# An attention and a feed-forward kernel: other loads, other engines and another order for batch 0

## The chip, the cores and the metric

The kernel runs on one core of a Trainium2 chip. The core has TensorE (PE, matmuls; PEld, the loading of their weights), VectorE (DVE), ScalarE (ACT), GpSimd (POOL) and SyncE (SP), and 16 DMA engines that all queues share. The metric is the time of one execution in device microseconds, the median of several runs. A profile comes from one further execution; its span is measured from the first instruction to the last.

## The reference

For each of 8 batches and 8 heads there are 576 tokens of 64 numbers in `q`, `k` and `v`, in fp32. `w_phi` is 64 x 128.

```python
def phi(x):
    proj = np.einsum('bhsd,df->bhsf', x, w_phi)
    proj = proj - np.max(np.abs(proj), axis=-1, keepdims=True)
    return np.concatenate([np.exp(proj), np.exp(-proj)], axis=-1)
q_p, k_p = phi(q), phi(k)
kv = np.einsum('bhsf,bhsd->bhfd', k_p, v)
z = np.sum(k_p, axis=2)
num = np.einsum('bhsf,bhfd->bhsd', q_p, kv)
den = np.einsum('bhsf,bhf->bhs', q_p, z)[..., None] + 1e-06
x = num / den                       # heads side by side: 4608 tokens x 512
out = (np.maximum(x @ w_gate, 0) * (x @ w_val)) @ w_out   # d_ff = 1536
```

## The kernel before

Every step of the work is a small function `do_xx`, and one long string, `ORDER`, lists the calls in the order in which they are issued. A word such as `ke.0.1.3.0:5@kp0` is step `ke` with arguments (batch 0, group of heads 1, chunk 3, sign 0), which works on PSUM bank 5 and takes slot 0 of the ring of buffers `kp`. Each engine takes its own instructions in the order of the words, and semaphores between the engines follow from the data. So the string sets what is queued behind what, on each engine, and on the DMA queues of SP, ACT and POOL.

The 576 tokens of a batch are split: 512 of them in four chunks of 128, and the last 64, which are packed with those of other heads or of another batch. Heads are loaded and worked on in three groups, (0,1), (2,3,4) and (5,6,7). For a group the steps are:

- `lk`, `lq`, `lm`, `ln` load k, q and the remainders on POOL's queue and turn fp32 into bf16 on the way. `lv` loads v; of batch 0 on POOL's queue, of the others on SP's. `lw` loads v's remainders on SP. `wl` and `wo` load thirds of the feed-forward weights on POOL's queue (`wl.0` is w_val, `wl.1` w_gate). `wp` and `wq` load w_phi on SP in two layouts, a 32-row and a 64-row one, and `wc` and `wd` turn them into bf16 on DVE.
- k is turned. In batch 0 TensorE does it (`k0`, transposes against the identity made by `id`, then the copy `k1` on DVE, then the product with w_phi, `k2`); in later batches DVE's 32x32 transposes do it (`kt`, `ku`, then the product `kr`). q is turned by DVE in all batches (`qt`), and its product with w_phi is `qc`, or in batch 0 eight separate `qs`, of 32 rows each.
- ACT takes the exponentials of both signs (`ke` for k, L563; `qe` for q, L709). DVE takes the maxima of the absolute values (`kx`, L571; `qx`, L717). The scale that follows from k's maxima (`kk`, `kp`) goes into v: `vs` on POOL (L618), `vd` and `vp` on DVE, `vr` for v's remainder on POOL (L637, four calls a batch), `vo` for the column of ones.
- `kv` (L658) is the product of k's features with v, and `kc` or `kd` copies it out. `qy`, `qz`, `qu`, `qw` turn q's maxima into scales. `nu` (L757) is the product of q's features with kv; `nt`, `nv`, `nr`, `nx` (L778, L788, L796, L800) add the two signs, divide, and leave 128 tokens of x. `xp` turns x on TensorE and `xa` or `xc` copies it; later `xt` turns it by DMA.
- The feed-forward part: `pv`, `pg` (L945) for quarters of batch 0, `fv`, `fg` (L916) for 512 tokens at once, `va`, `vb`, `pa`, `pc` copy the value on ACT or DVE, `ga`, `pb` (L937, L966) multiply with the gate; `fo`, `fp` (L977, L1006) are the last product, `oc`, `oe` copy it and `od` stores it from SP.

`zz.n` issues n matmuls on a tile of zeros, on whatever bank the word names; nothing reads them. `gt.0` loads a few bytes from k of batch 0 on SP, so that what SP issues later waits for them.

The end of the string starts the last products; ahead of them, for most of the time, the words interleave the feed-forward part of one batch with the attention of the next.

Of the kernel before, what the change touches and what calls it, by code (L numbers as in the profile page):

```python
# [1066 lines left out]
```

## Time and profile before

| | |
|---|---|
| runs | 379.55, 379.31, 379.26 us; median 379.31 |
| profiled execution | 378.79 us, span 376.8 |
| granted TensorE clock, mean | 0.986 |
| TensorE busy | 367.3 us (97%) |
| DVE, ACT, POOL busy | 296.3, 222.6, 161.4 us |
| DMA | 38.04 MB moved |

The profiled execution took 2.0 us more than its span, and 0.5 less than the median of the runs. A matmul's busy time is modelled and overlaps its neighbours, so 97% is not 97% of the peak rate. Idle time of an engine other than the one that sets the end costs nothing by itself.

### The profile page before, as it was taken

The page shows a single profiled execution, that of the slowest core. Times are in us where ns is not written, and L with a number is a line of the kernel's source. Part 1 is how long each engine was busy: PE and PEld are TensorE (multiplying, and loading weights), DVE is VectorE, ACT ScalarE, POOL GpSimd, SP SyncE. Part 2 cuts the span into 40 slices and gives each one's busy share as a digit, 9 for nine tenths or more (in the row PEclk, how much of TensorE's full clock was granted, in tenths as well). Part 3 has the DMA queues.
Part 4 walks back from the last instruction along what each step waited for, and adds up shares of the span by engine and source line. Part 5 has one row for each costly group of instructions (what it writes and reads, how often), then busy time and mean ns, then how long its engine had stood idle before and what let it go on. Part 6 is the DMA issues. An engine that isn't in the chain of part 4 may idle for free.

```text
span 376.8 us, 9181 instructions
## 1 busy us (share of the span) xinstructions
PE 367.3 (97%) x3591; PEld 197.2 (52%) x3591; DVE 296.3 (79%) x680; ACT 222.6 (59%) x539; POOL 161.4 (43%) x180
## 2 busy tenths in 40 slices
PE   8788999999999999999999999999999999999996
...
PEclk9859999999999999999999999999999999999999
DMA  9999999699954664289713944193400021301122
...
DMA packets 90513, 38.04 MB, mean 101 GB/s; under 512 B 64230, under 2 KB 85734, under 8 KB 90470
## 3 DMA queue, kind: packets, MB, share of 16 engines
...
q10 hardware_dynamic: 144, 0.13, 0.1%
q14 instruction: 15, 0.12, 0.1%
...
## 4 chain that ended last, share of the span: by engine, by line
PE 89%; DVE 5%; ACT 4%; DMA 2%; issue 0%; SPq 0%; DVEq 0%; ACTq 0%
PE bank L916 46%; PE bank L977 22%; PE bank L658 6%; PE bank L757 4%; PE bank L945 4%; PE bank L694 3%; ACT kp L563 2%; PE bank L511 2%; DMA w64f<-in_w_phi_dram 2%; DVE mk L571 1%; ACT qp L709 1%; PE bank L1006 1%; PE bank L898 1%; DVE u L788 1%; DVE maxq L717 1%; DVE t L778 1%
## 5 line engine op out<-in xcount | busy, mean ns | idle before, releaser
L563 ACT ACTIVATE kp<-bank 128x384 bf16<-128x384 f32 x192 | 83.2, 513 | 26.2 <-PE bank L511 15.0
L977 PE MATMUL bank<-wo,h 128*128 128x512 bf16 x420 | 98.3, 379 | 0.0
L937 DVE SCALAR_TENSOR_TENSOR h<-bank,val 128x512 bf16<-128x512 f32 x100 | 66.3, 681 | 29.8 <-PE bank L916 25.5
L916 PE MATMUL bank<-xTs,wg 128*128 128x512 bf16 x352 | 86.7, 379 | 0.0
L916 PE MATMUL bank<-xTs,wv 128*128 128x512 bf16 x352 | 86.2, 379 | 0.0
L800 POOL TENSOR_TENSOR xu<-u,r 128x512 bf16<-128x512 f32 x36 | 37.5, 1044 | 97.3 <-DVE r L796 92.4
L931 ACT CAST val<-bank 128x512 bf16<-128x512 f32 x70 | 41.6, 606 | 62.2 <-PE bank L916 50.8
L709 ACT ACTIVATE qp<-bank 128x512 bf16<-128x512 f32 x128 | 70.9, 632 | 10.1 <-DVE maxq L717 5.1
L618 POOL TENSOR_TENSOR vs<-vn,ek 128x780 bf16<-128x780 f32 (+3 forms) x40 | 53.0, 1338 | 37.8 <-ACT ek L580 35.1
L977 PEld LDWEIGHTS <-h 128*128 128x128 bf16 x420 | 39.1, 98 | 44.0 <-issue 0.9
L916 PEld LDWEIGHTS <-wv 128*128 128x128 bf16 x400 | 37.0, 98 | 43.2 <-issue 3.5
L916 PEld LDWEIGHTS <-wg 128*128 128x128 bf16 x400 | 37.4, 98 | 42.0 <-issue 1.8
L571 DVE TENSOR_REDUCE mk<-bank 128x3 f32<-128x384 f32 x96 | 49.0, 539 | 4.3 <-ACT kp L563 2.2
L717 DVE TRANSPOSE_TENSOR_REDUCE maxq<-bank 128x16 f32<-128x512 f32 x64 | 42.3, 692 | 3.5 <-PE bank L694 2.3
L986 ACT COPY ob<-bank 128x512 f32<-128x512 f32 x23 | 13.6, 593 | 37.5 <-PE bank L977 37.2
L788 DVE TENSOR_TENSOR u<-bank,t 128x195 f32<-128x195 f32 (+1 forms) x108 | 33.4, 330 | 1.9
L778 DVE TENSOR_TENSOR t<-bank,cq 128x195 f32<-128x195 f32 (+1 forms) x96 | 29.8, 327 | 5.0 <-PE bank L757 4.1
L757 PEld LDWEIGHTS <-qp 128*128 128x128 bf16 x512 | 24.1, 98 | 13.6 <-issue 2.0
L757 PE MATMUL bank<-kv,qp 128*128 128x65 bf16 x512 | 27.2, 194 | 1.2 <-ACT qp L709 0.8
L934 DVE CAST val<-bank 128x512 bf16<-128x512 f32 x30 | 20.2, 678 | 8.4 <-PE bank L916 8.3
L658 PEld LDWEIGHTS <-kp 128*128 128x128 bf16 x640 | 24.0, 101 | 3.7 <-DVE h L937 0.3
L658 PE MATMUL bank<-vs,kp 128*128 128x65 bf16 x512 | 24.2, 199 | 0.0
...
## 6 DMA issues: line engine op xcount, KB each, us to landing
...
```

The costliest lines, as they stand in the source:

```text
L563: nc.scalar.activation(kp_of(3 * b + j)[:, i, s].rearrange("p n f -> p (n f)"), bank[bk[0]][:, 0 : 3 * F], AF.Exp, scale=(1.0, -1.0)[s],)
L571: nc.vector.tensor_reduce(mk_of(3 * b + j)[:, :, i], bank[bk[0]][:, 0 : 3 * F].rearrange("p (n f) -> p n f", f=F), axis=AX.X, op=ALU.max, ...
L618: nc.gpsimd.tensor_tensor(vs_of(3 * b + j)[:, s, 0:n].rearrange("p n i e -> p (n i) e")[:, :, 0:e], src[:, lo:hi].rearrange("p h i e -> p ...
L658: nc.tensor.matmul(out_ps[:, h - lo, s, :], lhsT=lhsT, rhs=rhs, start=(at == 0), stop=(at == 2 * n * (C + 1) - 1),)
L709: nc.scalar.activation(qp_of(4 * b + i)[:, s, 4 * hq : 4 * hq + 4].rearrange("p h m -> p (h m)"), bank[bk[0]], AF.Exp, scale=(1.0, -1.0)[s],)
L717: nc.vector.tensor_reduce(maxq[:, :, i, 4 * hq : 4 * hq + 4].rearrange("p t h -> p h t"), bank[bk[0]].rearrange("p (h t u) -> p h t u", h= ...
L757: nc.tensor.matmul(bank[bk[0]][:, E * n : E * (n + 1)], lhsT=qp_of(4 * b + i)[:, s, h, :], rhs=kv_of(b)[:, h, s, :],)
L800: eng.tensor_tensor(xu_of(n).rearrange("p (h d) -> p h d", d=D), u_of(n)[:, :, 0:D], r_of(n).to_broadcast([P, H, D]), op=ALU.mult,)
L916: nc.tensor.matmul(bank[bk[0]], lhsT=w[:, dc, P * f : P * f + P], rhs=xT(g)[:, dc, :], start=(dc == 0), stop=(dc == NDC - 1),)
L931: nc.scalar.copy(val_of(NFC * g + f), bank[bk[0]])
L937: nc.vector.scalar_tensor_tensor(h2_of(g, f), bank[bk[0]], 0.0, val_of(NFC * g + f), op0=ALU.max, op1=ALU.mult)
L977: nc.tensor.matmul(bank[bk[0]], lhsT=h2_of(g, f)[:, P * t : P * t + P], rhs=wo_sb[:, f, :], start=(f == 0), stop=(f == NFC - 1),)
```

## The change

Nearly the whole string stands in another order, and some steps are replaced:

- k's group 1 of batch 0 (heads 2 to 4) is loaded by SP as fp32 (`lf`, into the space of `xT_mix`), and turned into bf16 by DVE (`cf.0`, two heads) and ACT (`cg.1`, one head), where `lk.0.1` did both on POOL's queue.
- w_phi is loaded once (`wr`, on ACT's queue, 64-row layout). Its 32-row copy is made by TensorE (`w1`, two matmuls with the selection matrix `sel`, which `sl` makes on DVE from the identity) and copied by ACT (`wa`). `wp`, `wq`, `wc` go.
- q of batch 0 is turned by TensorE (`q0`, 16 transposes in all) and copied by DVE (`q1`), and its product with w_phi is `qb`, eight matmuls of 64 rows and 512 columns, in place of `qt` and `qs` (16 matmuls of 32 rows and 512 columns). Tokens of a tile of batch 0 are then every fourth token, so `od` of batch 0 stores rows with a stride.
- `vr` (four calls a batch) becomes `vq` (two calls a batch of twice the size), in all batches.
- The matmuls on zeros are 71 in 14 places in place of 62 in 5; nearly all write bank 1.
- `id` comes ahead of POOL's first load. `wl.0.1` comes ahead of two of the three loads of v of batch 0; `lk.1.3` and `lq.1.2` ahead of two `vs`; `wl.1.0` behind all `vs` of batch 0. `gt.0` goes; a `gt.1`, which reads the buffer `kT`, stands near the end. A few copies change between ACT and DVE.

The string up to the first `pv`, before and after:

```diff
-ms.0 ms.2 ms.3@vr0 lk.0.1 ms.6 wp wq ms.4@vr1 wd ms.5 lq.0.1 wc id if zz.37:0 k0.1:0 k1.1:0@kT0
-zz.5:1 k2.1:0123 lk.0.2 ke.0.1.1.0:1@kp0 ke.0.1.2.0:2 ke.0.1.3.0:3 ke.0.1.0.0:0 qt.0.1@qT0
-ke.0.1.3.1:3 kx.0.1.1:1@mk0 lk.0.0 kx.0.1.2:2 ke.0.1.2.1:2 ke.0.1.1.1:1 lm.0.1 zz.6:4 k0.2:4
-k1.2:4@kT0 zz.7:5 k2.2:4567 ke.0.2.2.0:6@kp1 kx.0.1.3:3 ke.0.2.3.1:7 lm.0.0 lq.0.0 kx.0.1.0:0
-kx.0.2.0:4@mk1 ke.0.1.0.1:0 lw.0.0 k0.0:2 k1.0:2@kT0 zz.7:1 k2.0:2013 kk.0.1.1@ek0 ke.0.2.1.1:5
-qt.0.0@qT1 kx.0.2.3:7 ke.0.2.2.1:6 kx.0.2.2:6 kx.0.0.0:2@mk2 lv.0.1 ke.0.0.2.1:1@kp2 ke.0.2.1.0:5
-lm.1.0 lv.0.0 ke.0.0.3.1:3 ke.0.0.1.0:0 ke.0.2.0.0:4 lv.0.2 ke.0.0.0.1:2 kk.0.1.0 lm.1.1 wl.1.0
-kx.0.2.1:5 kp.0.2.1:7 ke.0.0.0.0:2 ke.0.2.0.1:4 lw.0.1 qs.0.1.0:6 kx.0.0.1:0 kx.0.0.3:3 qx.0.1.0:6
-vs.0.1.1@vs0 kp.0.2.0:7 qs.0.0.1:5 qe.0.0.1.0:5@qp0 gt.0 lk.1.3 qs.0.0.2:2 lv.1.2 kx.0.0.2:1
-ke.0.2.3.0:7 vp.2:7@vs1 kk.0.0.1@ek1 vs.0.1.0 ke.0.0.2.0:1 qs.0.0.0:4 wl.0.1 kk.0.0.0 ke.0.0.3.0:3
-qx.0.0.0:4 qx.0.0.2:2 vo.0@vs2 vd.0.2.0:7 ke.0.0.1.1:0 qs.0.1.1:1 qe.0.0.1.1:5 qe.0.0.0.1:4@qp1
-qx.0.1.1:1 qs.0.1.2:3 qe.0.1.2.0:3@qp2 qe.0.0.0.0:4 qs.0.0.3:0 qe.0.0.3.0:0@qp3 wl.0.0 qe.0.1.0.0:6
-qs.0.1.3:4 qx.0.0.1:5 qe.0.0.3.1:0 vd.0.2.1:7 qe.0.1.0.1:6 qe.0.1.1.0:1 vr.0.0.0 vr.0.0.1 qy.0.0:5
-qx.0.1.2:3 vr.0.1.0 qx.0.1.3:4 vr.0.1.1 kv.0.2:7 kc.0.2:7@kv0 vo.1 kv.0.1:6 qz.0.0:5@my0 qu.0.0@mz0
-qw.0.0@cq0 qx.0.0.3:0 kt.1.1@kT0 nu.0.0.2:7 nt.0.0.2:7@t0 qe.0.1.3.1:4 qy.0.1:0 qz.0.1:0@my0
-vs.0.0.1 kc.0.1:6 ku.1@kT1 vs.0.0.0 kv.0.0:5 qe.0.1.3.0:4 nu.0.0.1:6 nt.0.0.1:6@t1 kc.0.0:5
-qe.0.0.2.0:2 qu.0.1@mz0 qw.0.1 qy.0.2:0 qe.0.1.1.1:1 nv.0.0.1:6@u0 qe.0.1.2.1:3 qy.0.3:4 nu.0.0.0:5
-nt.0.0.0:5@t2 qe.0.0.2.1:2 nv.0.0.2:7 nv.0.0.0:5 nr.0.0@r0 nu.0.1.1:1 qz.0.2:0@my0 qu.0.2@mz0 lv.1.0
-nt.0.1.1:1@t2 qz.0.3:4@my0 nu.0.1.2:5 qw.0.2 nv.0.1.1:1@u1 lq.1.2 nt.0.1.2:5@t0 kr.1.1:7630
-nx.0.0@xu0 ke.1.1.3.1:0@kp2 wl.1.1 ke.1.1.0.0:7 nu.0.1.0:2 nt.0.1.0:2@t2 nu.0.2.0:4 xp.0.0:1
-xa.0.0:1 nv.0.1.2:5 nv.0.1.0:2 wo.0 nu.0.2.1:5 nr.0.1@r0 nx.0.1@xu0 kx.1.1.3:0@mk2 wl.0.2 nu.0.2.2:2
-lm.2.0 nt.0.2.1:5@t2 ke.1.1.3.0:0 nt.0.2.2:2@t0 nt.0.2.0:4@t1 ke.1.1.1.1:6 lm.2.1 qu.0.3@mz0
-kx.1.1.2:3 pv.1.0:1 pa.1.0:1@val0 ke.1.1.1.0:6 nv.0.2.0:4@u1 nv.0.2.1:5 nv.0.2.2:2 nr.0.2@r0
 ...
+ms.0 ms.3@vr0 wr ms.5 ms.4@vr1 id sl lf cf.0 if wd lk.0.2 cg.1 zz.17:0 k0.1:0 k1.1:0@kT0 lq.0.0
+lm.0.0 lk.0.0 lm.0.1 zz.2:1 w1:2 lq.0.1 lm.1.1 wa:2 zz.2:1 k2.1:0345 ke.0.1.3.0:5@kp0 kx.0.1.1:3@mk0
+ke.0.1.2.1:4 lv.0.1 k0.2:2 kx.0.1.3:5 ke.0.1.0.1:0 kx.0.1.2:4 k1.2:2@kT1 ke.0.1.3.1:5 wl.0.1
+ke.0.1.2.0:4 zz.3:1 q0.0:6 lv.0.0 ms.2 q1.0:6@qT0 zz.4:1 k2.2:4257 ke.0.1.1.1:3 zz.2:1 k0.0:6
+ke.0.1.0.0:0 kx.0.2.1:2@mk1 lv.0.2 ke.0.1.1.0:3 ke.0.2.0.1:4@kp1 ke.0.2.1.1:2 kx.0.1.0:0 k1.0:6@kT1
+kk.0.1.1@ek0 kx.0.2.3:7 kx.0.2.0:4 lw.0.0 kk.0.1.0 ke.0.2.1.0:2 ke.0.2.2.1:5 ke.0.2.3.1:7 zz.8:1
+k2.0:6032 ke.0.0.3.1:2@kp2 kx.0.2.2:5 ke.0.2.0.0:4 zz.7:1 q0.1:4 kx.0.0.2:3@mk0 kx.0.0.3:2
+ke.0.2.2.0:5 qb.0.2:5 lm.1.0 kx.0.0.1:0 ke.0.0.2.0:3 q1.1:4@qT1 ke.0.0.3.0:2 vs.0.1.0@vs0 lw.0.1
+ke.0.0.2.1:3 ke.0.0.1.0:0 vo.1 kp.0.2.1:7 lk.1.3 kp.0.2.0:7 ke.0.0.1.1:0 zz.2:1 qb.0.0:2 kx.0.0.0:6
+qb.1.0:4 qe.0.1.0.1:4@qp0 lq.1.2 vs.0.1.1 qx.0.0.2:5 ke.0.2.3.0:7 ke.0.0.0.1:6 kk.0.0.1@ek1
+vs.0.0.1@vs1 kk.0.0.0 vo.0 vq.0.1 qe.0.1.0.0:4 qe.0.0.2.1:5@qp1 qb.1.1:3 qx.0.0.0:2 qx.0.1.1:3
+vp.2:7@vs2 qe.0.1.1.0:3@qp2 zz.2:1 qb.0.1:0 qx.0.0.1:0 qx.0.1.0:4 ke.0.0.0.0:6 qe.0.0.2.0:5
+qe.0.0.1.0:0 vd.0.2.0:7 vq.0.0 lw.1.0 zz.15:1 qy.0.0:4 qz.0.0:4@my0 zz.2:1 qb.0.3:6 qe.0.1.1.1:3
+vd.0.2.1:7 qb.1.3:5 qe.0.0.0.1:2 qu.0.0@mz0 lw.1.1 qb.1.2:4 qx.0.1.3:5 qe.0.0.1.1:0 qe.0.0.0.0:2
+zz.3:1 kv.0.1:3 qx.0.0.3:6 qx.0.1.2:4 kc.0.1:3@kv0 qe.0.0.3.1:6@qp3 kv.0.2:0 qy.0.3:3 nu.0.0.1:2
+qw.0.0@cq0 kc.0.2:0 wl.0.0 vs.0.0.0 kv.0.0:7 wl.1.0 qe.0.1.2.0:4 kc.0.0:7 lv.1.2 lv.1.3 kt.1.1@kT1
+qy.0.2:0 nt.0.0.1:2@t0 qz.0.3:3@my0 qe.0.0.3.0:6 nv.0.0.1:2@u0 qz.0.2:0@my1 qy.0.1:3 qz.0.1:3@my2
+nu.0.0.2:1 nt.0.0.2:1@t0 nu.0.0.0:0 qu.0.1@mz0 nt.0.0.0:0@t1 nv.0.0.2:1 nv.0.0.0:0 nr.0.0@r0
+nx.0.0@xu0 qe.0.1.3.1:5 zz.2:2 kr.1.1:7236 qe.0.1.2.1:4 qu.0.2@mz1 nu.0.1.2:1 qw.0.1 qe.0.1.3.0:5
+nu.0.1.1:0 kx.1.1.2:3@mk0 lv.1.0 nt.0.1.2:1@t1 nu.0.1.0:4 nt.0.1.0:4@t0 xp.0.0:5 nt.0.1.1:0@t2
+ke.1.1.1.1:2@kp2 ke.1.1.2.1:3 nv.0.1.0:4@u0 lv.1.1 qu.0.3@mz0 wl.1.1 nv.0.1.1:0 nu.0.2.1:4
+nu.0.2.2:0 qw.0.2 nv.0.1.2:1 nr.0.1@r0 nt.0.2.1:4@t1 nt.0.2.2:0@t2 nv.0.2.1:4@u1 nu.0.2.0:1
+nt.0.2.0:1@t0 nx.0.1@xu0 nv.0.2.2:0 nv.0.2.0:1 wl.0.2 ke.1.1.1.0:2 xa.0.0:5 pv.1.0:5 ke.1.1.2.0:3
 ...
```

The functions:

```diff
@@ -343,11 +342,11 @@
     xT_all = sb.tile([P, 4, NDC, SF], BF16, name="xTs", tag="xTs")
     xT_mix = sb.tile([P, NDC, SF], BF16, name="xTm", tag="xTm")
     h2 = sb.tile([P, NH2, SF], BF16, name="h2", tag="h2")
-    w32f = sb.tile([P, 2, F], FP32, name="w32f", tag="w32f")
     w64f = sb.tile([P, F], FP32, name="w64f", tag="w64f")
     w32 = sb.tile([P, 2, F], BF16, name="w32", tag="w32")
     w64 = sb.tile([P, F], BF16, name="w64", tag="w64")
     ident = sb.tile([P, P], BF16, name="ident", tag="ident")
+    sel = sb.tile([D, 2, P], BF16, name="sel", tag="sel")
     identf = sb.tile([P, P], FP32, name="identf", tag="identf")
     zero = sb.tile([P, 256], BF16, name="zero", tag="zero")
     mark = sb.tile([P, D], BF16, name="mark", tag="mark")
@@ -369,17 +368,33 @@
 
 
 
-    def do_wp(bk):
-        nc.sync.dma_start(
-            out=w32f.rearrange("p a f -> p (a f)"),
-            in_=w_phi.rearrange("(r a) f -> r (a f)", a=2)[None].to_broadcast([4, R, 2 * F]),
-        )
+    def do_sl(bk):
+        nc.vector.tensor_copy(
+            sel.rearrange("d a (i r) -> d a i r", r=R),
+            ident[0:D, 0:D].rearrange("d (r a) -> d a r", a=2)[:, :, None, :].to_broadcast([D, 2, 4, R]),
+        )
+
+    def do_w1(bk):
+        for a in range(2):
+            nc.tensor.matmul(
+                bank[bk[0]][:, F * a : F * (a + 1)],
+                lhsT=sel[:, a, :],
+                rhs=w64[0:D, :],
+                start=(a == 0),
+                stop=(a == 1),
+            )
 
     def do_wq(bk):
         nc.sync.dma_start(out=w64f, in_=w_phi[None].to_broadcast([2, D, F]))
 
+    def do_wr(bk):
+        nc.scalar.dma_start(out=w64f, in_=w_phi[None].to_broadcast([2, D, F]))
+
     def do_wc(bk):
-        nc.vector.tensor_copy(w32.rearrange("p a f -> p (a f)"), w32f.rearrange("p a f -> p (a f)"))
+        nc.vector.tensor_copy(w32.rearrange("p a f -> p (a f)"), bank[bk[0]][:, 0 : 2 * F])
+
+    def do_wa(bk):
+        nc.scalar.copy(w32.rearrange("p a f -> p (a f)"), bank[bk[0]][:, 0 : 2 * F])
 
     def do_wd(bk):
         nc.vector.tensor_copy(w64, w64f)
@@ -419,6 +434,31 @@
             in_=k[b, lo:hi, 0:SF, :].rearrange("h (p c) d -> p h c d", c=C),
         )
 
+    def k_first():
+        flat = xT_mix.rearrange("p a b -> p (a b)").bitcast(FP32)[:, 0 : 3 * C * D]
+        return flat.rearrange("p (h x) -> p h x", h=3)
+
+    def do_lf(bk):
+        lo, hi = HEADS[1]
+        nc.sync.dma_start(
+            out=k_first().rearrange("p h (c d) -> p h c d", d=D),
+            in_=k[0, lo:hi, 0:SF, :].rearrange("h (p c) d -> p h c d", c=C),
+        )
+
+    def cast_first(copy, half):
+        lo, hi = ((0, 2), (2, 3))[half]
+        at = HEADS[1][0]
+        copy(
+            kn_of(0)[:, at + lo : at + hi].rearrange("p h c d -> p h (c d)"),
+            k_first()[:, lo:hi],
+        )
+
+    def do_cf(bk, half):
+        cast_first(nc.vector.tensor_copy, half)
+
+    def do_cg(bk, half):
+        cast_first(nc.scalar.copy, half)
+
     def do_lq(bk, b, hq):
         lo, hi = (4 * hq, 4 * hq + 4) if hq < 2 else (0, H)
         nc.gpsimd.dma_start(
@@ -461,9 +501,18 @@
                 in_=v[b, :, P * i : P * i + P, :].rearrange("h p d -> p h d"),
             )
 
+    def do_lu(bk, i):
+        lo, hi = HEADS[i]
+        nc.sync.dma_start(
+            out=v_flat()[:, lo:hi],
+            in_=v[0, lo:hi, 0:SF, :].rearrange("h (p c) d -> p h c d", c=C),
+        )
+
     def do_gt(bk, j):
 
-        nc.sync.dma_start(out=mark[0:1], in_=kn_of(0)[0:1, HEADS[j][0], 0, :])
+        nc.sync.dma_start(
+            out=mark[0:1], in_=kT_of(j).rearrange("p n m a -> p (n m a)")[0:1, 0:D]
+        )
 
     def do_lw(bk, b, hh):
         nc.sync.dma_start(
@@ -638,6 +687,15 @@
             vr_of(b)[r, s, :, hh, :],
             vm_of(b)[r],
             ek_of(3 * b)[r, s, 0, :][:, :, None].to_broadcast([SM, 4, E]),
+            op=ALU.mult,
+        )
+
+    def do_vq(bk, b, hh):
+        r = slice(SM * hh, SM * (hh + 1))
+        nc.gpsimd.tensor_tensor(
+            vr_of(b)[r, :, :, hh, :],
+            vm_of(b)[r][:, None, :, :].to_broadcast([SM, 2, 4, E]),
+            ek_of(3 * b)[r, :, 0, :][:, :, :, None].to_broadcast([SM, 2, 4, E]),
             op=ALU.mult,
         )
 
@@ -679,6 +737,30 @@
 
 
 
+    def do_q0(bk, hq):
+        pt = bank[bk[0]].bitcast(BF16)
+        for n in range(8):
+            h, cp = 4 * hq + n // 2, n % 2
+            nc.tensor.matmul(
+                pt[:, P * n : P * n + P],
+                lhsT=qn_of(0)[:, h, 2 * cp : 2 * cp + 2, :].rearrange("p c d -> p (c d)"),
+                rhs=ident,
+                is_transpose=True,
+            )
+
+    def do_q1(bk, hq):
+        nc.vector.tensor_copy(
+            qT_of(hq).rearrange("p h m a -> p (h m a)"), bank[bk[0]].bitcast(BF16)
+        )
+
+    def do_qv(bk, hq):
+        nc.scalar.copy(qT_of(hq).rearrange("p h m a -> p (h m a)"), bank[bk[0]].bitcast(BF16))
+
+    def do_qb(bk, hq, i):
+        T = qT_of(hq).rearrange("p h m a -> p (h m a)").rearrange("p (h k m) -> p h k m", k=2, m=P)
+        r = slice(D * (i % 2), D * (i % 2 + 1))
+        nc.tensor.matmul(bank[bk[0]], lhsT=w64[r, :], rhs=T[r, :, i // 2, :], start=True, stop=True)
+
     def do_qt(bk, b, hq):
         dst = qT_of(2 * b + hq).rearrange("p h m a -> p (h m a)").bitcast(FP32)
         src = qn_of(b)[:, 4 * hq : 4 * hq + 4].rearrange("p h c d -> p (h c d)").bitcast(FP32)
@@ -991,6 +1073,8 @@
     def do_od(bk, g, t):
         if g < B:
             dst = out[S * g + P * t : S * g + P * (t + 1), :]
+            if g == 0:
+                dst = out[0:SF, :].rearrange("(p c) n -> p c n", c=C)[:, t]
             nc.sync.dma_start(out=dst, in_=ob_of(4 * g + t))
             return
         for bb in range(2):
```

More of the change, by code (lines that the diff above doesn't have):

```diff
@@ new lines @@
+ku.7@kT1 ke.6.2.2.0:2 nr.8.2@r2 qx.6.0.1:5 kt.7.0 od.3.0 oe.4.3:6@ob2 qe.6.0.2.0:1 xt.5.3
+ke.6.2.2.1:2 fo.4.0.0:3 fo.4.0.1:3 fo.4.0.2:3 oe.4.0:3@ob0 nx.5.1@xu3 xt.5.1 nx.5.2@xu1 xt.5.2
+fv.5.4:2 vb.5.4:2@val0 qe.6.0.1.1:5 qc.6.1:5673 qe.6.0.3.1:4@qp0 qe.6.0.3.0:4 qx.6.1.2:7
+qe.6.1.3.0:3 qx.6.0.2:1 fv.5.0:4 va.5.0:4@val2 od.4.3 qx.6.0.0:0 qe.6.1.2.1:7 fg.5.4:2 lv.6.2
+vs.6.2.0@vs2 ga.5.4:2@hs7 fv.5.9:4 va.5.9:4@val0 kk.6.2.1 vs.6.2.1 vs.6.0.0@vs1 vs.6.1.1@vs0
+vs.6.1.0 qe.6.1.3.1:3 vs.6.0.1 lv.7.0 lw.7.0 fg.5.0:1 fo.4.2.0:4 fo.4.2.1:4 qx.6.1.3:3
```

427 lines of the change are left out of this document (210 added, 217 removed).

## The prediction

> **What bounds the kernel now.** First the page's busy slices (40 slices of 9.4 us each):
>
> ```profile
> PE   8788999999999999999999999999999999999996
> ...
> PEclk9859999999999999999999999999999999999999
> DMA  9999999699954664289713944193400021301122
> ```
>
> From the fifth slice on TensorE is full at full clock. Only the first four slices (38 us) and the last one have holes, and there the granted clock falls to 5 tenths. DMA is full for the first seven slices. So the end is "when TensorE gets its first unlimited work" plus a fixed sum of work. The sum from rows at full clock: 1220 matmuls of 128x512 at 0.216 us are 263 us, 1280 of 128x65 at 0.95/30 are 41, 256 of L945 at 0.89/16 are 14, the rest some 29, together 347 without the zero matmuls. Some 9 us of these are done when the first L945 starts at 32.1; the other 338 would end at 370.2, and the last matmul ends at 373.6. So in 340 us only 3.4 are lost, and the last output takes 3.2 more. What the new order changes late can hardly win anything; what it changes before 32 us counts in full. So the second view is the chain of waits, in its first 40 us (start, length, what):
>
> ```profile
> 1.56 6.35 DMA w64f<-in_w_phi_dram
> ...
> 9.72 3.95 ACT kp L563 x10
> ...
> 23.50 3.30 PE bank L658 x60
> ...
> 27.18 0.65 PE bank L658 x20
> ...
> 32.32 0.89 PE bank L945 x16
> ```
>
> w_phi lands at 7.9, features of k (L563) run from 9.72, the k-v products (L658) from 23.3, the feed-forward part (L945) from 32.1. The 60 products take 55 ns each, the later 20 take 33: half clock. The windows of 3.41 us show where it was lost (PE busy is the second figure; PEclk, DMA share and GB/s close the row):
>
> ```profile
> 9.73:13.14 3.41, 3.24 (x44) 2.50 (x43) 3.40 (x7) 3.41 (x9) 2.91 (x4) 1.00 1.23 270
> 13.14:16.55 3.41, 1.59 (x20) 0.70 (x19) 3.41 (x8) 3.41 (x11) 1.53 (x2) 1.00 1.04 228
> 16.55:19.96 3.41, 2.97 (x9) 0.59 (x10) 3.10 (x7) 3.41 (x14) 3.37 (x5) 0.50 1.20 195
> 19.96:23.38 3.42, 2.48 (x10) 0.63 (x7) 3.12 (x5) 3.42 (x9) 3.26 (x8) 0.50 1.39 197
> 23.38:26.79 3.41, 3.41 (x65) 3.41 (x64) 3.05 (x6) 2.17 (x6) 2.92 (x4) 0.50 1.23 203
> ```
>
> After a window with 1.59 us busy the clock was halved; it came back behind a full window. DVE and ACT (third and fourth pairs) are full from 10 to 23. Who gates the products at 23.3 is in the timeline:
>
> ```profile
> 14.29 1.47 POOL L618 TENSOR_TENSOR vs<-vn,ek 128x768 bf16<-128x768 f32 x1 [1.09 <-DMA vn<-in_v_dram]
> ...
> 20.66 2.48 POOL L637 TENSOR_TENSOR vr<-vm,ek 64x260 bf16<-64x260 f32 x4
> ...
> 22.17 0.92 DVE L600 TENSOR_TENSOR vs<-vn,bank 128x768 bf16<-128x768 f32 x1
> ```
>
> Both chains end together: POOL's at 23.14, DVE's at 23.09.
>
> **Step 1, the start of the features.** Before: 9.72, behind w64f. After, k's heads 2 to 4 come as fp32 on SP. They cannot land before 0.74 (issue) + 2.2 (an SP write of 256 KB) + 0.4 for the other 128 KB = 3.3, nor do I expect them after 6.35, where the same heads land now (issue 1.25, 5.1 us). From the first DMA bytes (2.3) and 393 KB at the 316 GB/s of the best 1-us row I get 3.55, plus some 0.7 to be told of: 4.3, nearer the lower end, since the identical slot of the queue is used and POOL's loads start later than now. Behind SP's load wait cf.0 on DVE (0.353 + 2 x 0.126 = 0.6, the casts of 256 and 128 columns continued) with `if`, `wd` and the first k1 queued behind it, and cg.1 on ACT (0.4, beside it) with `wa` and all features behind. Then six transposes 0.5, k1 0.54, k2 to first feature 0.5: 6.5. Handovers and a TensorE still at half clock (17 zero matmuls instead of 37 end at about 4.7) add up to 1: **7.5**, bounds 6.5 and 9.6. w_phi's 32-row copy (`sel` 0.3 on DVE, two matmuls, `wa` 0.4 on ACT) fits into k1's time; if it were late, `wa` would delay the first feature by its whole 0.4. w64f's one load, on ACT's queue ahead of the 1.28-us table load, has until 5.4 to land. The memsets and `sel` lie where DVE now idles 4.6 us for w64f.
>
> **Step 2, DVE to its last v scaling.** Now from the first L571 at 10.34 to 23.09: 12.75. Added: two copies of 128x1024 (0.54 x 1024/768 = 0.72 each), one qz 0.25, a memset 0.06; gone: one L685 of 1.09 and 0.3 of waiting. 13.1, so 7.55 + 13.1 = **20.7** instead of 23.1. ACT: 24 features (0.38 each by the chain's steps), 8 small ones at 0.1, ten L709 at 0.51 are 15: 22.6 instead of 24.5.
>
> **Step 3, POOL.** The identity moves ahead of the first load: 0.6 later, but one load (1.25 us of the queue by the landings 9.37 and 10.62) leaves it. v's heads 2 to 4 land at 14.14 now; I take 13.8. wl.0.1 (512 KB, 3 us of the queue) now lies ahead of v's other heads, which land near 17.5 and 18.7 instead of 15.5 and 16.6. POOL then runs vs 1.47, vo 0.29, lk.1.3 0.94, lq.1.2 0.95, vs 1.49, vs 1.03, vo 0.27 and two vq. The trace has no vq (64x520). It costs between 0.62 and 1.24 (one and two L637); I take 1.05, the row of L618 with as many elements in a partition (128x520). Sum 13.8 + 8.55 = **22.35**, instead of 23.14. So POOL, not DVE, is late next: of the 2.4 us of step 2 only 0.8 is left here, since POOL waits for v, and v for the one shared set of DMA engines. lq.1.2 (25.35 now, 16.5 then) and lk.1.3 stand ahead of two vs: 1.9 us of this chain. gt.0 on SP goes; lv.1.2 now waits there behind lw.1.1, until vq has read vm.
>
> **Step 4, the clock.** The 60 products cost 3.3 at half clock and 1.9 at full: 1.4. In 13.14 to 16.55 I count for the new order: the last of k2.0 and zz.7 0.5, eight turns of q 0.45, four zeros 0.4, four qb 0.9: 2.2 instead of 1.59, of full or 64-row matmuls instead of 32-row ones; then 15 zeros (1.6, or 3.2 at half clock: nearly a full window, the kind that brought the clock back). I take full clock. The Trainium skill, "TensorE: Matmul & The Clock Gate", section "Why this matters for your kernels", asks only for no idle gaps over about 3 us; here the longest gap before the fall was 1.30 us, so the trace disagrees. Its Part 4 holds that transposes do not count as busy, which speaks against the turns of q; no row here shows it.
>
> **Step 5, to the feed-forward part.** The products run 22.35 to 24.3; vs.0.0.0 ends at 24.25; the last 20 products end at 25.35 instead of 27.85. From there to L800 and L945 the same chain (4.3 us): L945 at 29.6 instead of 32.1, **2.5 us** earlier. q's turns and qb against qs on TensorE (0.9 + 1.7 against 3.5) lie beside DVE's stretch and count nothing; if that cover goes, 0.9 comes back. The batch-0 output rows are strided but as many; gt.1, a load of 0.1 KB, now lies in SP's queue near the end, where SP waits anyway. Vq in later batches and the other placing of val and output copies lie off TensorE's full stretch. I keep 0.1 for them. Profiled execution: 378.79 (span 376.8 + 2.0) - 2.4 = 376.4; the median of the runs is 0.5 above the profiled one: **376.9**.
>
> **Rivals.** A measurement of this kernel can tell 0.2%, 0.76 us, from no change.
> *Clock halved anyway.* For it: the count of 2.2 is no full window either, and the zeros are few. Then the products end at 25.7, the last 20 at about 27.0: gain 0.85, 378.5.
> *k lands no earlier.* Landing 6.35 puts the features at 9.5: DVE ends at 22.7, ACT at 24.6; POOL's 22.35 stays, and the rest is about 0.8 later: gain 1.6, 377.7. The Trainium skill, "DMA: Bandwidth & Descriptors", section "Issuing engines are not separate DMA queues", says that another issuing engine saves issue time alone; by that rule this is the case. Against it: the load goes out half a microsecond earlier and with nothing ahead.
> *Gate weights late (slower).* wg's first third lands at 20.92 now, used at 33.23. After, wl.1.0 is issued behind vs.0.0.0, at 24.3, behind k, q and wv. Loads of 512 KB in the full queue took 7.6 to 12.4: landing 31.9 to 36.7. TensorE comes to pg.0.1 at about 33.3, and waits in order. From 35.7 on the gain is gone; at 36.7 the stall is 3.4: 380.3. For it: DMA is full. Against: SP's v loads of batch 2, which ran beside the 12.4, come later.
> *The new order loses later.* DVE is 96 to 99% busy in 35 to 60; an order that feeds it worse adds to the 3 us lost there now; twice that: 379.9 to 381.
> Both of the first two together leave some 0.5, no change that can be told; that lies within the clock's "same".
>
> **Numbers.** Forecast 0.42, clock 0.20, k no earlier 0.12, gate weights 0.13, later losses 0.13. Faster: 0.42 + 0.12 + half of the clock case + 0.02 of small stalls = 0.66. Same: the other half and 0.03 = 0.13. Slower: 0.21. The forecast's own range is 375.3 (vq at 0.62, features at 6.5) to 377.9; reaching to the gate weights, 375.3 to 380.5.
>
> **What would show it.** Right: first L612 near 7.5, no lower clock between 16.5 and 26.8, first vq behind two vs, the products (L716 or so) at 22 to 24.5 with 32 ns each, pv near 29.6, TensorE full behind. Wrong: a PE wait on DMA wg or wv at 30 to 37; 55 ns per product; cf.0 waiting past 6; PE holes after 40 us.

## The result and the profile after

The kernel after takes **377.37 us** (median of 9 runs, 376.35 to 378.53) against 379.26 (9 runs, 378.15 to 379.81): a ratio of 0.9954, 95% interval 0.994 to 0.9968. The profiled execution takes 377.2 us (span 375.4) against 378.79 (span 376.8). So it is faster, by 1.9 us where 2.4 were forecast. Times are medians of runs in one state: of the eleven runs of e10 below, two (385.1 and 385.4 us) fell in a slower state, at a lower granted clock, and are left out. The busy slices of its page, 9.4 us each:

```profile
PE   7989999899999999999999999999999999999996
...
PEclk9999999999999999999999999999999999999999
DMA  9999996858977918562936496054312012300223
```

The clock no longer falls in the first four slices, and TensorE is fuller in the second and the fourth; but its eighth slice (66 to 75 us) is no longer full. Both are followed up below. The chain of waits, first 40 us (start, length, what):

```profile
2.36 6.48 DMA qn<-in_q_dram
...
10.99 0.49 ACT kp L612
...
19.36 1.05 POOL vr L695
...
21.59 1.93 PE bank L716 x56
...
23.85 0.63 PE bank L716 x20
```

w_phi is gone from the chain. 56 of the k products take 1.93 us, 34 ns each, where they took 55; the last 20 end at 24.5 instead of 27.8. The windows of 3.41 us that answer to those shown of before:

```profile
13.14:16.55 3.41, 2.82 (x21) 1.22 (x18) 3.41 (x8) 3.38 (x11) 3.38 (x4) 1.00 0.95 254
16.55:19.96 3.41, 2.79 (x20) 1.82 (x20) 3.36 (x7) 3.41 (x11) 3.33 (x5) 1.00 1.18 143
19.96:23.38 3.42, 2.99 (x67) 2.30 (x66) 3.42 (x7) 3.35 (x8) 3.33 (x5) 1.00 1.30 169
```

TensorE is busy 2.8 us where it was 1.59, and the clock stays at 1.00. The starts of the steps, from the timeline:

```profile
7.04 4.44 ACT L612 ACTIVATE kp<-bank 128x384 bf16<-128x384 f32 x10 [0.40 <-PE bank L603]
...
13.17 1.48 POOL L667 TENSOR_TENSOR vs<-vn,ek 128x768 bf16<-128x768 f32 x1 [1.85 <-DMA vn<-in_v_dram]
...
19.36 2.18 POOL L695 TENSOR_TENSOR vr<-vm,ek 64x520 bf16<-64x520 f32 x2
```

Features start at 7.04 instead of 9.72, and the feed-forward part (L1027) at 28.76 instead of 32.16: 3.4 us earlier. At the end 1.4 us of the span are left of that. Where the rest goes stands in the timeline of TensorE and in the sums of its waits (in all, times, longest) between 60 and 200 us:

```profile
73.72 0.59 PE L998 MATMUL bank<-xTs,wv 128*128 128x512 bf16 x2 [0.82 <-DMA xTs<-xu]
```

```profile
PE bank L998 <- DMA xTs<-xu: 1.0, 2, 0.8
```

TensorE comes to the first matmul of the next group (fv, L998) before its x tile, which a DMA transpose (xt, L899) brings. In the trace of before the first fv of group 1 does not wait for x. Its tile landed at 73.52, and in the chain of waits the matmul follows other matmuls:

```profile
73.69 1.83 PE bank L977 x8
75.53 1.73 PE bank L916 x8
```

So x was there 2.0 us ahead of TensorE. In the kernel after TensorE is done with what comes before at 72.9, 2.6 us earlier. The tile's last transpose also leaves earlier, at 69.57 instead of 71.08, but it takes 4.01 us instead of 2.45 and lands at 73.58. With 2.45 us it would have landed at some 72.0, ahead of TensorE (an estimate from these rows). So the hole comes from the longer transfer. The DMA traffic while it is on its way, in the kernel after and then in e1 (below), where the same transpose takes 2.42 us:

```profile
q1 hardware_dynamic: 1128, 0.27, 58.2%
q8 instruction: 1, 0.02, 2.0%
...
xTs<-xu SPq DMA_TRANSPOSE x1, 4.0
```

```profile
q1 hardware_dynamic: 1039, 0.25, 53.2%
...
xTs<-xu SPq DMA_TRANSPOSE x1, 2.4
```

In neither stretch does a packet of an output or of GpSimd's queue run. The one other thing beside the long transpose is a packet of some 16 KB in the queue that the profile calls `instruction`; it begins at 70.86, in the middle of the transfer. The same tile was slow with such a packet in e3 (4.12), e8 (3.78), e9 (4.12), e12 (4.60) and e13 (4.28), and took 2.4 us without one in before, e1, e2, e6, e7, e10 and e11; in e5 one began only in the last 0.1 us, and the transpose took 2.42. So the packet and the long transfer go together in all 14 traces. What makes the packet come there, and how it costs so much, stays open.

To follow a lead through the run, I add up TensorE's work from the records of its weight loads (each with the time of its matmul, zero matmuls with none, the 1.6 us of q's turns and the like taken off) and compare two kernels at one time. The sums are good to some 0.3 us. Microseconds ahead:

| at us | 30 | 60 | 75 | 120 | 200 | end |
|---|---|---|---|---|---|---|
| after, of before | 2.4 | 3.2 | 2.1 | 2.0 | 1.0 | 1.5 |

Three single holes of TensorE stand in these stretches, 0.95 us at 73.7, 0.58 at 113.8 and 0.71 at 188.4, each ahead of the first fv of a group (counted between weight loads; the idle times that the profile itself gives are shorter, 0.82, 0.23 and 0.37). Counted the same way, the largest hole of before in that part is 0.31.

### The profile page after: what moved, and what is told of

It reads as the page before. It is cut to its first block, busy times and chain, and to the rows that moved or that the text cites. A ratio compares the mean times of both kernels' runs of the same rounds, so it can differ in the third digit from the quotient of the medians.

```text
span 375.4 us, 9157 instructions
## 1 busy us (share of the span) xinstructions
PE 362.0 (96%) x3558; PEld 196.2 (52%) x3610; DVE 294.2 (78%) x677; ACT 225.5 (60%) x545; POOL 157.7 (42%) x163
## 4 chain that ended last, share of the span: by engine, by line
PE 84%; DVE 5%; DMA 3%; POOL 3%; issue 2%; ACT 2%; SPq 0%; DVEq 0%; POOLq 0%; ACTq 0%
PE bank L998 43%; PE bank L1059 21%; PE bank L716 5%; PE bank L839 4%; PE bank L1027 4%; PE bank L560 2%; PE bank L776 2%; DMA qn<-in_q_dram 2%; DVE mk L620 1%; DVE t L860 1%; DVE u L870 1%; DMA xTs<-xu 1%; DVE h L1019 1%; POOL xu L882 1%; ACT kp L612 1%
## 5 line engine op out<-in xcount | busy, mean ns | idle before, releaser
L1059 PE MATMUL bank<-wo,h 128*128 128x512 bf16 x403 | 96.3, 379 | 1.2 <-issue 0.5
L1019 DVE SCALAR_TENSOR_TENSOR h<-bank,val 128x512 bf16<-128x512 f32 x100 | 67.2, 682 | 35.4 <-ACT val L1013 16.9
L998 PE MATMUL bank<-xTs,wg 128*128 128x512 bf16 x335 | 86.7, 379 | 1.2 <-issue 0.3
L998 PE MATMUL bank<-xTs,wv 128*128 128x512 bf16 x337 | 85.0, 379 | 2.1 <-DMA xTs<-xu 1.0
L791 ACT ACTIVATE qp<-bank 128x512 bf16<-128x512 f32 x128 | 70.1, 617 | 7.0 <-DVE maxq L799 4.1
L998 PEld LDWEIGHTS <-wv 128*128 128x128 bf16 x400 | 37.1, 98 | 42.8 <-issue 3.7
L998 PEld LDWEIGHTS <-wg 128*128 128x128 bf16 x400 | 36.9, 98 | 41.2 <-issue 1.1
L839 PEld LDWEIGHTS <-qp 128*128 128x128 bf16 x512 | 24.4, 98 | 13.1 <-issue 0.9
L695 POOL TENSOR_TENSOR vr<-vm,ek 64x520 bf16<-64x520 f32 x16 | 16.8, 1053 | 21.2 <-ACT ek L629 17.6
L716 PEld LDWEIGHTS <-kp 128*128 128x128 bf16 x640 | 22.3, 98 | 3.4 <-ACT qp L791 0.4
```

The costliest lines, as they stand in the source:

```text
L716: nc.tensor.matmul(out_ps[:, h - lo, s, :], lhsT=lhsT, rhs=rhs, start=(at == 0), stop=(at == 2 * n * (C + 1) - 1),)
L791: nc.scalar.activation(qp_of(4 * b + i)[:, s, 4 * hq : 4 * hq + 4].rearrange("p h m -> p (h m)"), bank[bk[0]], AF.Exp, scale=(1.0, -1.0)[s],)
L839: nc.tensor.matmul(bank[bk[0]][:, E * n : E * (n + 1)], lhsT=qp_of(4 * b + i)[:, s, h, :], rhs=kv_of(b)[:, h, s, :],)
L998: nc.tensor.matmul(bank[bk[0]], lhsT=w[:, dc, P * f : P * f + P], rhs=xT(g)[:, dc, :], start=(dc == 0), stop=(dc == NDC - 1),)
L1019: nc.vector.scalar_tensor_tensor(h2_of(g, f), bank[bk[0]], 0.0, val_of(NFC * g + f), op0=ALU.max, op1=ALU.mult)
L1059: nc.tensor.matmul(bank[bk[0]], lhsT=h2_of(g, f)[:, P * t : P * t + P], rhs=wo_sb[:, f, :], start=(f == 0), stop=(f == NFC - 1),)
```

## Experiments

Two theories of where the gain comes from stood at the start. One is the prediction's: k's early arrival, then v on GpSimd, then the clock, each counting in full. The rival: what TensorE wins in the head is taken back where it waits for x. A second rival came up with e2: not k but w_phi held the features. The ratios are to the kernel before in the same session, whose median was 378.5 to 379.4 us; from one session to another they compare better than the times.

**No fill (e1).** All zero matmuls but the first 17 leave the order:

```diff
-zz.2:1 (twice) zz.3:1 zz.4:1 zz.2:1 zz.8:1 zz.7:1 zz.2:1 (twice) zz.15:1 zz.2:1 zz.3:1 zz.2:2
```

> The kernel after with the 54 zero matmuls of the head taken out, all but the first 17; everything else as it is. Theory (the fill holds the clock): the busy time of TensorE in the windows of 13.1 to 23.4 us falls from 2.8 to 3.0 us to some 1.6 to 2.3, the granted clock goes to 0.5 somewhere from 13 to 20 us and comes back at 24 to 27, the k products of L716 take 1.4 us more than the 1.93 of the kernel after, and the time is 377.9 to 378.8 us (1.4 less up to half of it, which later waits for x may hide). Rival (the fill is idle work; the turns of q by TensorE and the 32-row copy keep the clock by themselves): the clock stays at 1.00, the products stay at 1.93 us and the time is 377.1 to 377.5.

Measured: 377.45 us (7 runs), ratio to before 0.9961 (0.9942 to 0.998): the same as with the fill. Yet the clock did fall, sooner than expected: at 7.11 instead of between 13 and 20; it was back at 24.18. Windows of e1:

```profile
6.31:9.72 3.41, 1.66 (x22) 1.23 (x23) 2.15 (x5) 3.18 (x9) 1.91 (x4) 0.62 1.54 186
...
16.55:19.96 3.41, 1.09 (x4) 0.03 (x1) 3.41 (x8) 3.40 (x11) 3.00 (x5) 0.50 1.22 148
```

Both theories had a half right. The mechanism holds (the zeros keep the clock), the price is not seen at the end: L1027 starts 1.45 us later (30.21), and against the kernel after, counted at the same matmul, e1 is 1.5 us behind at 60 us, 0.6 at 75, 0.2 at 120 and 0.3 ahead from 190 on. In e1 the first fv of group 1 runs at 74.29 behind other matmuls, with no wait:

```profile
73.98 0.38 PE L980 MATMUL bank<-kv,qr 128*64 128x65 bf16 x12
74.29 1.04 PE L998 MATMUL bank<-xTs,wv 128*128 128x512 bf16 x4
```

So of the 1.5 us that e1 is behind, the kernel after spends 0.9 waiting for x at 73.7, some 0.4 by 120 and 0.5 at 188.4, at its three holes. The intervals of the two ratios leave some 0.9 us either way; that the clock is worth nothing at all is not shown. Runs on record speak against it: two of e1's seven kept a mean clock of 1.00 and took 376.24 and 377.15 us, the other five (0.977 to 0.981) have a median of 377.49; of the kernel before, 17 runs at 0.991 have a median of 378.43 and 49 at 0.985 or 0.986 one of 379.21.

**k by SyncE, alone (e2).** The kernel before with this part only:

```diff
-ms.0 ms.2 ms.3@vr0 lk.0.1 ms.6 wp wq ms.4@vr1 wd ms.5 lq.0.1 wc id if zz.37:0
+ms.0 ms.3@vr0 lf wp wq ms.5 ms.4@vr1 id lq.0.1 cf.0 if wd wc ms.2 ms.6 cg.1 zz.17:0
```

> The kernel before with one part of the change alone: k's first three heads are read in fp32 by SyncE ahead of the weights and cast by VectorE and ScalarE, and the first fill is 17 zeros instead of 37. Theory (k's arrival gates ScalarE and VectorE, then v on GpSimd and the slow clock are next): the first exponential of k is at 7.0 to 7.6 us instead of 9.72, ScalarE and VectorE are 2 us earlier, GpSimd's last v product stays at 22.5 to 23.2 us, the clock still halves and the products take 3.3 us; the first gate products come 0.9 to 1.6 us earlier than 32.16, and the time is 377.7 to 378.5. Rival 1 (k is no gate): time as before, 379.1 to 379.5. Rival 2 (k is the only gate): all of the lead, 3 us or more, is there with k alone, and the time is 376.2 to 377.5.

Measured: 383.11 us (6 runs), ratio 1.0117 (1.0096 to 1.0137): 4.6 us **slower**, and no theory had that. The timeline of e2:

```profile
4.17 0.55 DVE L436 CAST kn<-xTm 128x512 bf16<-128x512 f32 x1 [0.85 <-DMA xTm<-in_k_dram]
...
10.22 0.25 DVE L385 CAST w<-w64f 128x128 bf16<-128x128 f32 x1 [5.38 <-DMA w64f<-in_w_phi_dram]
...
12.03 2.79 ACT L588 ACTIVATE kp<-bank 128x384 bf16<-128x384 f32 x7 [7.45 <-PE bank L579]
```

and its window (TensorE, weight loads, VectorE, ScalarE, GpSimd):

```profile
6.31:9.72 3.41, 0.00 (x0) 0.00 (x0) 0.00 (x0) 0.00 (x0) 1.77 (x4) 1.00 1.43 185
```

k is there at 4.17, but w_phi, now behind it on SyncE and beside the loads of q and k, is there at 10.2 instead of 7.9: features at 12.03, and three engines with nothing to do before. So w_phi is what the features wait for, in the kernel before too, whose timeline shows it: its VectorE idles 4.60 us for w64f until 7.94, while k has landed at 6.35.

```profile
7.94 0.23 DVE L385 CAST w<-w64f 128x128 bf16<-128x128 f32 x1 [4.60 <-DMA w64f<-in_w_phi_dram]
```

**k back on GpSimd, in the kernel after (e3).**

```diff
-ms.0 ms.3@vr0 wr ms.5 ms.4@vr1 id sl lf cf.0 if wd lk.0.2 cg.1
+ms.0 lk.0.1 ms.3@vr0 wr ms.5 ms.4@vr1 id sl if wd lk.0.2
```

> The kernel after with its k part undone: the first three heads of k are read first in GpSimd's queue, cast by the transfer, as before; the two casts fall out. Theory (k gates the head): the first exponential of k goes from 7.0 to 9.2 to 9.8 us, ScalarE's chain to the first kc ends 2 us later, the first products of L1027 come at 30.3 to 31.2 instead of 28.8 us and the time is 378.3 to 379.3. Rival (GpSimd's chain of v sets the end): the head moves by no more than the 1 us that one more issue puts v back, and the time is 377.4 to 378.0.

Measured: 377.36 us (8 runs), ratio 0.9963 (0.9946 to 0.998). The same as the kernel after. The features start at 7.76, not at 9.2 to 9.8:

```profile
4.73 0.23 DVE L400 CAST w<-w64f 128x128 bf16<-128x128 f32 x1 [1.01 <-DMA w64f<-in_w_phi_dram]
...
6.01 0.51 PE L582 MATMUL bank<-ident,kn 128*128 128x128 bf16 x6 [1.15 <-DMA kn<-in_k_dram]
```

With w64f at 4.73 (5.66 in the kernel after, beside the fp32 load of k), k is next at 5.96, and its move to SyncE is worth 0.72 us of the start and nothing at the end. The expectation's rival came out, but not for its reason: GpSimd's chain ended 0.3 us later, as all of the head did.

**The weight part alone, and with k (e6, e7).** The kernel before with w64f in ScalarE's queue and the 32-row copy by TensorE, w32f's load gone (and a first fill short enough for the earlier start); then k's part as well. The first of the two:

```diff
-ms.0 ms.2 ms.3@vr0 lk.0.1 ms.6 wp wq ms.4@vr1 wd ms.5 lq.0.1 wc id if zz.37:0 k0.1:0 k1.1:0@kT0 zz.5:1
+ms.0 ms.2 ms.3@vr0 wr lk.0.1 ms.6 ms.4@vr1 id sl ms.5 if wd lq.0.1 zz.25:0 k0.1:0 k1.1:0@kT0 zz.2:1 w1:4 wa:4 zz.2:1
```

> The kernel before with the weight part of the change alone: w64f by one load in ScalarE's queue, the 32-row copy made by TensorE, no load of w32f; k's first heads stay in GpSimd's queue, cast by the transfer, and the first fill is 25 zeros. Theory W (w_phi's arrival holds the features of the kernel before, since k lands there at 6.35 and the cast of w64f comes at 7.94): the first exponential of k comes at 7.4 to 8.4 us instead of 9.72, the first gate products at 30.4 to 31.4 instead of 32.16, and the time is 0.7 to 1.7 us under the kernel before. Rival (the lead that the change keeps does not come from the start of the features; before's order of v, the slow clock and its later queue take it): features as early, gate products at 31.6 or later, time within 0.5 us of before.

> As the weight part alone, and k's first three heads in fp32 by SyncE with the two casts, behind nothing, as in the kernel after; the first fill is 17 zeros. Theory W: the first exponential is at 6.9 to 7.4 us, 0.5 to 0.9 earlier than with the weights alone, which the later steps of the head take up: the time is within 0.4 us of the weight part alone. Rival (with the weights in time k is worth its own 1 to 2 us): 0.8 us or more below the weight part alone.

Measured: the weights alone 377.5 us (6 runs, 377.33 to 377.79), ratio 0.9951 (0.9938 to 0.9963): all of the change's gain that is left at the end, in before's order, with v in its old place and q's turns on VectorE. The gain of 1.9 us is a little more than the 0.7 to 1.7 expected. With k 377.1 (6 runs), ratio 0.9939 (0.9926 to 0.9952), within 0.4 as expected and not told apart; its features start at 7.13, 0.26 before those of the weights alone, where 0.5 to 0.9 was expected. Timeline of the weights alone:

```profile
4.73 0.27 DVE L398 CAST w<-w64f 128x128 bf16<-128x128 f32 x1 [0.91 <-DMA w64f<-in_w_phi_dram]
...
7.39 2.02 ACT L601 ACTIVATE kp<-bank 128x384 bf16<-128x384 f32 x5 [0.34 <-PE bank L592]
```

Its L983 (the feed-forward part) starts at 31.0, and its lead over before is 1.2 us from 30 on and 1.3 at the end: smaller than the change's in the head, and kept, for no group waits for x there. Its clock still halves (0.50 in 16.55 to 23.38).

**The gate weights later (e8).** `wl.1.0` moves behind `nx.0.0` in GpSimd's queue.

> The kernel after with one word of GpSimd's queue moved: wl.1.0, the first third of the gate weights, stands behind nx.0.0 and so goes out 4 us later, at 27.6 instead of 23.3 us; wl.1.1 follows it. It lands at 35.5 to 37.0 instead of 32.7, and TensorE, which comes to pg.0.1 at 33.2, waits 2.3 to 3.8 us. Theory (the head has 1.4 us to spare against the x tiles of the next group, as the kernel without fill showed): 0.9 to 2.4 us of it are left at the end, time 378.3 to 379.8. Rival 1 (every microsecond of TensorE counts): 379.7 to 381.2. Rival 2 (the head has 3 us or more to spare): 377.2 to 377.8.

Measured: 378.94 us (11 runs), ratio 0.9986 (0.9972 to 1.0), 1.6 us above the kernel after (1.2 by the ratios). The time is where the theory had it, the way there is not. The first third landed at 33.62 and the second, behind it, at 37.97; the waits from 30 to 42 us:

```profile
PEld L1027 <- DMA wg<-in_moe_w_gate_dram: 1.4, 2, 0.7
```

The landing was 2 to 3 us earlier than expected and TensorE waited for both thirds, 0.7 each, 1.4 where 2.3 to 3.8 was expected. The lead fell by 1.0 us at 60 and was still down 0.9 at 120; another 0.9 went at 190, where x's tile, 7.2 us on its way, was 1.62 late. So a loss in the head counts in part, what the x tiles take differs from kernel to kernel by as much, and the right time was partly luck.

**The x tiles (e5, e9, e12, e13).** Four moves of single words on SyncE or GpSimd:

```diff
 e5:  xt.1.0 behind nx.1.0, od.0.1 behind xt.1.3, xt.3.0 behind nx.3.0
 e9:  xt.1.0 behind nx.1.0, od.0.1 behind oc.0.1
 e12: lq.6.2 behind vq.5.0
 e13: as e12, and lm.3.1 behind lk.3.3
```

> The kernel after with three words of SyncE's queue in another order: the transposes xt.1.0 and xt.3.0 stand directly behind the steps that make their source, and the output od.0.1 stands behind xt.1.3. Nothing else moves. Theory (the lead of the head is given back where TensorE reaches the first matmul of a group before its x tile is there): the 0.95 us stall at 73.7 us goes down to 0.1 to 0.4 and the 0.58 us one at 113.8 to under 0.2; the time is 375.9 to 376.7. Rival (the tile is not what is late, or another of the same group lands as late; the lead is lost to the work itself): stalls of the same size a little later, time 377.2 to 377.6.

> The kernel after with two words of SyncE's queue moved: the output od.0.1 stands behind oc.0.1, ahead of the transposes of batch 1, where the queue idles, and xt.1.0 directly behind nx.1.0. No buffer comes free later than in the kernel after. Theory (the x tile of group 1 is late by SyncE's order and by the 4.0 us of its last transpose): the last transpose of batch 1 goes out at 68.3 to 68.7 instead of 69.57 us and lands at 70.9 to 72.7, the stall of 0.95 us at 73.7 goes, and the time is 376.3 to 377.0. Rival (the next group's tile takes it back at 113): stall gone, one of 1.0 to 1.5 us at 113, time 377.1 to 377.6.

> The kernel after with one word of GpSimd's queue moved: lq.6.2 (512 KB of q) stands behind vq.5.0, so that it goes out at 184.2 instead of 182.16 us, behind the transpose xt.4.2, which now lands 6.32 us after its issue at 182.03. Theory (the load beside it makes the transpose late): xt.4.2 lands at 184.5 to 186.6, the stall of 0.71 us at 188.4 goes, and the time is 376.6 to 377.1. Rival (the outputs in SyncE's queue or an instruction fetch make it late, or the next wait takes it): time 377.2 to 377.7.

> The kernel after with lq.6.2 behind vq.5.0, and one more word of GpSimd's queue moved: lm.3.1 (32 KB of k in small packets) stands directly behind lk.3.3, at 60.9 instead of 63.86 us, where GpSimd waits two microseconds for VectorE, and no longer runs beside the x transposes of batch 1. Theory (small loads beside the transposes make the tile of group 1 late): the last transpose of batch 1 lands under 73.0 us, the stall of 0.95 us at 73.7 falls under 0.5, and the time is 375.6 to 376.3. Rival (the 512 KB of k ahead of them, the output od.0.1 or an instruction fetch make them late): stall and landing as they are, time 376.3 to 376.9, as with lq.6.2 moved alone.

e5: 379.54 us (12 runs), ratio 1.0019 (1.0001 to 1.0037), 2 us slower than the kernel after (2.5 by the ratios). The tile of group 1 landed at 70.97, as hoped, but the output od.0.1 left later, and the waits from 70 to 76 us show what hung on it:

```profile
ACT ob L1068 <- DMA out_dram<-ob: 1.9, 1, 1.9
PE bank L998 <- ACT ob L1068: 1.8, 1, 1.8
```

oc.0.3 writes the buffer that od.0.1 was still reading, and the first fv writes the bank that oc.0.3 had to empty. Neither theory had this; a word moved in a queue has to be followed to the readers and writers of its buffer.

e9: 377.22 us (6 runs), ratio 0.9933 (0.9912 to 0.9953). The last transpose went out at 69.62, not at 68.3 to 68.7, and took 4.12 us; the hole at 73.8 was still 0.61. Neither theory came out as worded, and the time cannot be told from the kernel after.

e12: 376.49 us (6 runs, 376.26 to 377.45), ratio 0.9933 (0.9919 to 0.9947). With the 512 KB of q two microseconds later, the transpose beside it took 2.94 us instead of 6.32 and the hole at 188 was gone, as the theory had it. The load alone does not settle it: with it in its old place the same transpose took 4.36 us in e1, 4.23 in e3 and 7.23 in e8. The packets of the `instruction` queue part these: e1 has the load and no such packet beside the transpose, e12 and e13 have such a packet and no load (2.94 and 2.99), and the kernel after, e5, e8 and e9 have both (6.32 to 7.23). In e3 the packet is there too, 1.2 us after the issue, and the transpose took 4.23 all the same. The median is the lowest of all kernels and just under the range of its theory, but its interval overlaps that of the kernel after, and in its profile a hole of 1.71 at 74.3 had grown by as much as the one at 188 had lost.

e13: 376.84 us (11 runs), ratio 0.9948 (0.9933 to 0.9962): no gain on e12. km landed at 67.74, the last transpose of batch 1 still took 4.28 us, and the hole at 73.6 was 0.62: it is not the small load that makes it late. Nor is it an output or k's load: in the kernel after none of their packets run in these 4 us. What e13 and the kernel after have there, and e1 has not, is a packet of the `instruction` queue.

**Fill in before's order (e10, e11).** With the weights and k, zero matmuls ahead of each `qs` step, in the bank that it writes:

```diff
-qs.0.1.0:6
+zz.4:6 qs.0.1.0:6
```

and so for all eight, with zz.6:5 ahead of qy.0.0; e11 has 8 and 10.

> The kernel before with the weight part and the k part of the change, and with fill in its stage of q: four zero matmuls ahead of each of the eight qs steps of batch 0, in the bank that the step is about to write, and six ahead of the first qy. Order and queues stay those of the kernel before. Theory (the slow clock costs 1.4 us where no x tile is waited for afterwards: before's order has its x tile of group 1 at 73.5 us and needs it at 75.5): the granted clock stays at 0.9 or more from 13 to 27 us, the 60 k products take 1.9 instead of 3.3 us, the first gate products come at 29.6 to 30.4 instead of 31.3, and the time is 375.4 to 376.4 us, below both kernels. Rival 1 (the zeros delay q by as much as the clock brings, 0.45 us each on a path that waits for ScalarE): time 376.9 to 377.8. Rival 2 (the clock falls all the same): 377 to 378.5.

> As with four zeros, but eight ahead of each qs step and ten ahead of the first qy. If four zeros hold the clock, eight add 0.45 us to each step of q for nothing: 0 to 1.5 us above the kernel with four. If four are too few, eight hold it, and the time is 375.4 to 376.6 us.

Measured: 378.55 us (9 runs), ratio 0.9983 (0.9972 to 0.9993), and 382.36 (4 runs), ratio 1.0084 (1.0071 to 1.0097). e10 is above the ranges of all its theories, and e11 is 3.8 us above e10, where up to 1.5 was expected. A window of e10:

```profile
16.55:19.96 3.41, 3.41 (x19) 1.28 (x20) 2.07 (x5) 2.89 (x9) 3.39 (x6) 1.00 1.30 209
```

The clock held in both. But four zeros took 0.61 us, not 0.45, TensorE became the bound of the stage of q (VectorE, the third pair, is busy 2.07 where e7 has 3.04), and the first qy came at 23.3 instead of 21.5: what the clock brought, the fill took. L983 starts at 31.37 against 31.32. The profiled runs of e7 and e10 are as close (378.15 and 378.29), but that of e7 is the slowest of its six; the medians are 1.5 apart, which these profiles do not explain. The kernel after does it better: it fills a bank of its own while it waits, and its turns and 64-row steps of q need less of VectorE.

## Why the prediction was right, and where not

The direction, and 1.9 us of the forecast's 2.4, came out; the steps behind it did so in part.

*Step 1*, the start of the features: 7.04 against 7.5 (lf landed at 4.09, forecast 4.3; cf.0 0.61, cg.1 0.41). The size was right. But the part that brings it is w_phi on ScalarE's queue without a second load (9.72 to 7.39 in e6); k by SyncE adds 0.3 (e7) or 0.7 (e3). The prediction showed the row of w64f, wrote "behind w64f", and then took the landing of k as the term. The **rival "k lands no earlier"** failed by the same step: it put the features at 9.5, and e3 measured 7.76. The Trainium skill, "DMA: Bandwidth & Descriptors", section "Issuing engines are not separate DMA queues", lets another issuing engine save only its issue time. In e3 the heads went out at 1.24 and landed at 5.96, in the kernel after at 0.74 and 4.09, so 0.5 of the 1.9 us is issue time; the rest also has fp32 in place of a cast, and no run parts the two. At the end the move is worth nothing that can be told (e3).

*Step 2*: VectorE's last v at 20.91 (forecast 20.7), the end of ScalarE's exponentials at 22.54 (22.6). The ends are right, in part by luck: VectorE's stretch took 13.9 us where 13.1 was forecast and ScalarE's 15.5 where 15.0 was, and the start 0.46 us earlier made up for it.

*Step 3*: v landed at 13.02 (13.8), a vq took 1.05 (1.05), and GpSimd ended at 21.54 (22.35): late next as said, but by 0.16 us only.

*Step 4*: the clock stayed full, as forecast, and the 1.4 us of the products are there. As a term of the sum they are not seen: e1 lost them and ended at the same time, within the 0.9 us that the intervals leave. On the rule of the Trainium skill, "TensorE: Matmul & The Clock Gate", section "Why this matters for your kernels" (no idle gaps over some 3 us), all these runs disagree: the clock halved in before, e1, e6 and e7, and the longest gap of TensorE until then was 1.30, 1.17, 1.30 and 1.30 us. How busy TensorE is in one window does not settle it either. Cut where the clock changes in each run, the last full window before the fall held 1.59 us of work in before (13.14 to 16.55), 1.74 in e6, 1.93 in e7 and 1.94 in e1, and one with 1.97 in e10 kept the clock; but so did one with 1.63 in e2 (3.86 to 7.27). So these traces give no threshold.

*Step 5*: the last 20 products ended at 24.48 (25.35) and L1027 started at 28.76 (29.6), so the head gained 3.4 us where 2.5 were forecast. That is the first mis-sized term. The second is the 0.1 kept for all the rest, which measured some 1.5 to 2. The sentence that failed is "what it changes before 32 us counts in full": it holds only while x's tiles are ahead of TensorE, and of before's trace I had not asked how far ahead they were (2.0 us at 75). x's own chain came forward by 1.5 us and TensorE by 2.6, which the slack would have covered; the last transpose, 1.6 us longer, used it up. That the two errors nearly cancel is luck; with the first alone the forecast would have been 376.0.

*Rivals.* The gate weights landed at 32.72, TensorE took them at 33.20: half a microsecond to spare, inside the forecast's 31.9 to 36.7; e8 shows what it costs to lose it. "The new order loses later" happened in part, 1.5 to 2 us of the 3 or more it asked for, by waits for x and not by VectorE's feed.

What e6 shows of the whole change: one of its parts, in the old order, gives 377.5. The rest of the new order wins some 2 us more in the head and gives it back at x. That the parts v in GpSimd's queue and q's turns by TensorE are worth nothing by themselves was not tried.
